# MoE experts: rows gathered one expert earlier, 16-bit splits and crossbar transfers ahead of the scatters

## The chip, the cores and the metric

The kernel runs on one core of one Trainium2 chip. The metric is the device time of the slowest core in microseconds (us); with one core that is this core's time. Times in the text are us.

## What is computed

Banded attention (4 batches, 8 heads, 768 positions, head size 64) feeds a mixture of 8 experts over the 3072 tokens that result. The attention part stands outside the change; the expert part is this, shortened:

```python
logits = x @ w_gate                       # x: (3072, 512)
expert_idx = np.argmax(logits, axis=1)    # one expert for each token
for i in range(N):                        # a list of tokens for each expert
    e = expert_idx[i]
    if counts[e] < capacity:
        disp[e, counts[e]] = x[i]
        ...
h = np.maximum(np.einsum('ecd,edf->ecf', disp, w1), 0.0)   # 512 -> 1024
y = np.einsum('ecf,efd->ecd', h, w2)                       # 1024 -> 512
out[i] = gate_w[i] * y[expert_idx[i], pos[i]]              # back to the token's row
```

## The kernel before

The attention's rows are written to memory (`xrows`), the router makes for each expert a list of the tokens that chose it, and the experts 0 to 7 then run one after the other. All float32 products are made of float32r halves: a tensor t is split into th (rounded) and tl = t - th, and a product is three matmuls (th*wh, th*wl, tl*wh).

**Rounds.** An expert is a loop over f = 0 to 7, called rounds here, each with 128 of the 1024 hidden units. TensorE does in round f first the second layer of round f - 2 (`second`, lines 739 to 741: three matmuls of 512 columns for each block of 128 tokens), then the first layer of round f (`layer1`, line 731: 12 matmuls, as wide as the expert has tokens, in steps of 32). Which width runs is decided on the chip by branches (`widths`, line 940); all engines pass these branches. Widths are 480, 416, 384, 416, 384, 416, 416 and 288 for the experts 0 to 7. Where the last block holds only 32 tokens, eight small matmuls (`beside`, line 955) do its second layer, half of them in round 5 and half at the end. What is left of an expert's second layer (`last`) runs in round 0 of the next expert: 18 matmuls of 512 columns for three whole blocks (24 for four), and the eight small ones.

**ScalarE and VectorE** work in the order written, for each round: `hidden` (hh, line 981 on ScalarE; hl, line 982 on VectorE; hr, line 984), then pieces, the splits of weights that are used two steps later (a step is two rounds; lines 141 and 142: a cast of ScalarE and a subtraction of VectorE; four in round 1, two in each of the rounds 2 to 7), then in the rounds 3 to 6 a `join` for one block of 128 token rows of the next expert: x (line 853, VectorE), xh (line 855, ScalarE), xl (line 856, VectorE). The next expert's first layer needs all four xh.

**The rows of the next expert.** `gather` makes four blocks. `fetch` issues four indirect transfers on GpSimd's queue (xg, line 345). `halves` then splits the float32 rows into 16-bit halves on GpSimd (flat, line 847, two buffers) and issues a crossbar transfer on SyncE's queue (DMA transpose, line 848) that writes them turned back into xg. There are four xg buffers. For the experts 2 to 7 all of that is written in round 1 of the expert before, with a `drain` of GpSimd (line 1032) between the four gathers and the four splits. Expert 1's rows are gathered in round 2 of expert 0, expert 0's by another way.

**Queues.** The order on all five engines is the order written (manual schedules), so GpSimd's and SyncE's queues are served in order. GpSimd's: the four scatters of the expert before (out_dram, line 871, written in round 0), the four gathers, the drain, the four splits. SyncE's: `fetch(step + 3)` at the start of each even round loads 1 MB of weights (four transfers of 256 KB, line 133: two of w1, called wr, with four buffers, and two of w2, called w2r), and the crossbar transfers stand between the loads of round 0 and those of round 2.

Of the kernel before, what the change touches and what calls it, by code (L numbers as in the profile page):

```python
# [11 lines left out]
F32R = mybir.dt.float32r  # L12
# [8 lines left out]
P = 128  # L21
# [8 lines left out]
def fused(ctx: ExitStack, tc, q, k, v, wg, w1, w2, out, shape, n_global, n_local, cap):  # L30
    nc = tc.nc
    B, H, S, D = shape
    DM, E = wg.shape
# [4 lines left out]
    KC = DM // P  # L38
    NF = FF // P
# [71 lines left out]
    T4 = FIXED * P  # L111
# [219 lines left out]
    def turn_rows(ps, rows):  # L331
        for c in range(KC):
            nc.tensor.transpose(ps[:, c, :], rows[:, c * P:(c + 1) * P], ident)
# [9 lines left out]
    def fetch_rows(pool, name, bufs, gi, n=N):  # L343
        xg = pool.tile([P, DM], F32, name=name, bufs=bufs)
        ld = nc.gpsimd.indirect_dma_start(out=xg, out_offset=None, in_=xrows[0:n],  # L345
                                          in_offset=bass.IndirectOffsetOnAxis(ap=gi.bitcast(U32), axis=0),
                                          bounds_check=n - 1, oob_is_err=False)
        return xg, ld
# [385 lines left out]
    def layer2(e, f, a, y, hh, hl):  # L734
        w = wparts[e * (NF // FP) + f // FP][1]
        w2h, w2l = w["h"], w["l"]
        t = slice(a * P, (a + 1) * P)
        fi = f % FP
        nc.tensor.matmul(y, hh[:, t], w2h[:, fi], start=f == 0, stop=False)  # L739
        nc.tensor.matmul(y, hh[:, t], w2l[:, fi], start=False, stop=False)  # L740
        nc.tensor.matmul(y, hl[:, t], w2h[:, fi], start=False, stop=f == NF - 1)  # L741
# [46 lines left out]
    gi = const.tile([P, E, FIXED], I32, name="gi")  # L788
# [5 lines left out]
    def list_rows():  # L794
        nc.vector.tensor_copy(tb.bitcast(I32)[:, :, :, 0].rearrange("p e a -> p (e a)"), held[:, 0])
        nc.vector.tensor_copy(tb[:, :, :, 1].rearrange("p e a -> p (e a)"), held[:, 1])
# [20 lines left out]
    def bankC():  # L817
        spare.append(spare.pop(0) or bank([P, DM]))
        return spare[-1]
# [3 lines left out]
    moe = mctx.enter_context(tc.tile_pool(name="moe", bufs=2))  # L823

    def gather(gi, rows=()):

        xh, xl = [moe.tile([P, KC, T4], F32R, name=n) for n in ("xh", "xl")]
        rows = list(rows)

        def fetch():  # L830
            for a in range(len(rows), FIXED):
                xg, ld = fetch_rows(moe, "xg", FIXED, gi(a))
                rows.append(xg)
            return ld

        def turn(a, ps=None):
            ps = (bankC() if ps is None else ps).rearrange("p (c t) -> p c t", c=KC)
            turn_rows(ps, rows[a])
            o = slice(a * P, (a + 1) * P)
            nc.scalar.copy(xh[:, :, o], ps)  # L840
            nc.vector.tensor_tensor(xl[:, :, o], ps, xh.bitcast(F32)[:, :, o], op=ALU.subtract)

        def halves(a):


            flat = moe.tile([P, 2 * DM], U16, name="flat")
            nc.gpsimd.tensor_copy(flat.rearrange("p (n f) -> p n f", n=2), rows[a].bitcast(U16).rearrange("p (f n) -> p n f", n=2))  # L847
            nc.sync.dma_start_transpose(out=rows[a].bitcast(U16).rearrange("p (c t) -> p c t", t=P), in_=flat)

        def join(a):  # L850
            o = slice(a * P, (a + 1) * P)
            x = moe.tile([P, KC, P], F32, name="x")
            nc.vector.tensor_copy(x.bitcast(U16).rearrange("p c (t n) -> p n c t", n=2),  # L853
                                  rows[a].bitcast(U16).rearrange("p (n c t) -> p n c t", n=2, t=P))
            nc.scalar.copy(xh[:, :, o], x)  # L855
            nc.vector.tensor_tensor(xl[:, :, o], x, xh.bitcast(F32)[:, :, o], op=ALU.subtract)
        return xh, xl, turn, fetch, halves, join

    out_scatters = []

# [72 lines left out]
    def widths(e):  # L933

        def among(lo, hi):
            if hi - lo == 1:
                yield FINE * (lo + FIRST_ARM)
                return
            mid = (lo + hi) // 2
            with tc.If(arms[e] > mid - 1) as more:  # L940
                yield from among(mid, hi)
            with more.Else():
                yield from among(lo, mid)
        yield from among(0, NV)
# [13 lines left out]
    def whole(w):  # L958

        return range(SURE, w // P + (w % P > 2 * GR))  # L960
# [7 lines left out]
    def fetch(step, after=()):  # L968
        if step < STEPS and step not in wparts:
            pieces[step] = raw_weights(step, moe, "wr", 4, after, plain)  # L970
# [18 lines left out]
    def load_arm(e):  # L989
        arms[e] = nc.values_load(arm[0:1, e:e + 1], engines=[PE], min_val=0, max_val=NV - 1)  # L990


    xs = gather(lambda a: gi[:, 0, a:a + 1], first["rows"])
    fetch(PREFETCH)
    got = xs[3]()
    first["rest"]()
    for t, n in zip(xs, ("xh", "xl")):
        nc.gpsimd.tensor_copy(t[:, :, START], first[n])
# [17 lines left out]
    for e in range(E):  # L1016
        xh, xl = xs[0:2]
        hs = hs0 if e == 0 else {}

        def second(fs, a, e=e, hs=hs):  # L1020
            for f in fs:
                layer2(e, f, a, y_ps[a], *hs[f][0:2])

        for f in range(NF):
            step = (e * NF + f) // FP
            if f % FP == 0:
                fetch(step + SPLIT + 1)
                split = pieces.pop(step + SPLIT, [])
            if f == 1 and 0 < e < E - 1:
                xs = gather(lambda a, e=e: gi[:, e + 1, a:a + 1])  # L1030
                xs[3]()
                nc.gpsimd.drain()  # L1032
                for a in range(FIXED):
                    xs[4](a)
            if f == 1 and e == E - 1:
                nc.gpsimd.drain()
                most = nc.values_load(nblk[:, E:E + 1], min_val=0, max_val=max(RB, FIXED + 1))
            if f == 2 and e == 0:
                xs = gather(lambda a, e=e: gi[:, e + 1, a:a + 1])
                xs[3]()  # L1040
                for a in range(FIXED):
                    xs[4](a)
                first["h"](first["held"])
                list_rows()
            if f == 4 and e + 1 < E:
                load_arm(e + 1)
            h = h_ps[f % 2]

            fs = (f - 2,) if f > 1 else ()
            for a in range(SURE):  # L1050
                second([i for i in fs if e > 0 or i >= EARLY], a)
            part = slice(FIRST * P if e == 0 and f < EARLY else 0, T4)
            for w in widths(e) if e > 0 or f > 1 else ():
                for a in whole(w):
                    second(fs, a)
                if f == 5:
                    beside(e, range(0, 4), w, hs)
                layer1(e, f, h, xh, xl, slice(part.start, w))
            hidden(hs, f, part)
            if f == 0 and last is not None:  # L1060
                last()
            if f == 3 and e == 0:
                to = take_beside(tb)
            if f == 5 and e == 1:
                count_blocks()
            for piece in () if f == 0 else split if f == 1 else split[2 * (f % FP):2 * (f % FP) + 2]:
                piece()

            turned = {4: (0,), 5: (1, 2), 6: (3,)} if e == 0 else {3: (0,), 4: (1,), 5: (2,), 6: (3,)}
            for a in turned.get(f, ()) if e + 1 < E else ():  # L1070
                xs[5](a)

        def last(e=e, second=second, hs=hs):
            for a in range(SURE):
                second((NF - 2,), a)
            for w in widths(e):
                beside(e, range(4, NF), w, hs)
                for a in whole(w):
                    second((NF - 2, NF - 1), a)
            rest = [finish(e, a, to[:, e, a - SURE], y_ps[a]) for a in range(SURE, FIXED)]  # L1080
            rest[0]()
            for a in range(SURE):
                second((NF - 1,), a)
                finish(e, a, first["tb"][:, a] if e == 0 and a < FIRST else tb[:, e, a], y_ps[a])()
            rest[1]()
# [127 lines left out]
```

## Time and profile before

| what | value |
|---|---|
| median of 3 runs | 528.46 us (528.44, 528.46, 533.24) |
| the profiled execution | 525.51 us, span 523.8 us |
| busy share of the span | TensorE 85%, VectorE 59%, ScalarE 55%, GpSimd 34% |
| mean granted TensorE clock | 0.957 |
| matmuls | 3943 |

The span is the time from the first to the last instruction of the profiled execution; 1.7 us of its time lie around it. Engines are named PE (TensorE), DVE (VectorE), ACT (ScalarE), POOL (GpSimd) and SP (SyncE) in the rows; a q behind a name is that engine's queue. Matmul records overlap, since matmuls are pipelined: the pace is read from start to start. A granted clock of 1.00 is 2.4 GHz, one of 0.50 is 1.2 GHz.

### The profile page before, as it was taken

The numbers are of one execution on the slowest core, as the hardware profiler recorded it, in microseconds if no ns is written. First come the engines' busy times: TensorE is split into PE (matmuls) and PEld (weight loads), VectorE is DVE, ScalarE is ACT, GpSimd is POOL, SyncE is SP. The second block draws the span as 40 slices with busy tenths as digits, with TensorE's granted clock in tenths as the row PEclk, the third lists the DMA queues.
The fourth block names the chain that finished last, engine by engine and source line by source line (L and its number), as shares of the span: only waits on it lengthen the run. The fifth ranks groups of instructions, "written<-read, shape, count | busy, mean of one in ns | idle before, by whom it ended". The sixth has DMA issues, their size and how long they took to land.

```text
span 523.8 us, 11549 instructions
## 1 busy us (share of the span) xinstructions
PE 447.7 (85%) x3943; PEld 367.3 (70%) x3943; DVE 308.1 (59%) x978; ACT 287.2 (55%) x799; POOL 178.7 (34%) x285
## 2 busy tenths in 40 slices
PE   6899999999998889959977897798579958986993
PEld 3777787877787778847865795677469746955781
DVE  6679899898764564436534551663365355516632
ACT  4989999998733345335523551562356245515642
POOL 6004456665347104410640162054106301530303
PEclk9999999999999999988996999799889979998998
DMA  9999689763349833484459338635843572376301
GB/s 253 303 339 300 201 235 310 227 202 98 103 145 288 175 109 112 122 201 167 136 83 256 109 117 145 215 132 104 217 147 125 92 253 103 128 127 217 130 6 51
DMA packets 79601, 88.79 MB, mean 170 GB/s; under 512 B 35537, under 2 KB 47825, under 8 KB 79476
## 3 DMA queue, kind: packets, MB, share of 16 engines
q1 hardware_dynamic: 73812, 72.31, 49.1%
q0 software_dynamic: 5120, 14.69, 8.8%
q8 instruction: 92, 1.51, 1.2%
q14 instruction: 33, 0.27, 0.2%
q10 hardware_dynamic: 544, 0.02, 0.1%
HBM read 67.06 MB, written 14.68 MB: 156 GB/s over the span
## 4 chain that ended last, share of the span: by engine, by line
issue 35%; PE 27%; POOL 11%; DMA 10%; DVE 7%; ACT 6%; POOLq 2%; SPq 2%; ACTq 0%; DVEq 0%
DMA xg<-flat 6%; POOL flat L847 4%; POOL xg L345 4%; PE bank L731 4%; PE bank L486 4%; PE bank L548 4%; PE bank L545 4%; DVE sc L462 3%; PE bank L524 2%; ACT sc L497 2%; DMA wr<-in_moe_w_dram 2%; POOLq L1032 2%; POOL out_dram L871 2%; PE bank L739 2%; PE bank L741 1%
## 5 line engine op out<-in xcount | busy, mean ns | idle before, releaser
L739 PE MATMUL bank<-w2h,hh 128*128 128x512 f32 x192 | 83.1, 433 | 41.1 <-ACT hh L981 37.8
L731 PE MATMUL bank<-xh,w1h 128*128 128x416 f32 (+5 forms) x272 | 92.4, 347 | 10.0 <-ACT xh L855 9.6
L731 PE MATMUL bank<-xh,w1l 128*128 128x416 f32 (+5 forms) x272 | 90.7, 341 | 0.0
L497 ACT ACTIVATE sc<-sc,mx 128x168 f32<-128x168 f32 (+1 forms) x192 | 80.1, 422 | 10.6 <-DVE mx L462 9.6
L871 POOL DMA_INDIRECT out_dram<-ysb,to x16 | 16.2, 1012 | 197.5 <-ACT ysb L863 195.1
L741 PE MATMUL bank<-w2h,hl 128*128 128x512 f32 x192 | 81.3, 423 | 1.3 <-DVE hl L982 0.5
L740 PE MATMUL bank<-w2l,hh 128*128 128x512 f32 x192 | 80.8, 421 | 0.0
L739 PEld LDWEIGHTS bank<-w2h,hh 128*128 128x128 f32 x192 | 38.5, 200 | 55.9 <-ACT hh L981 41.9
L142 DVE TENSOR_TENSOR w1l<-wr,w1h 128x512 fp32r<-128x512 f32 x58 | 38.1, 692 | 61.1 <-ACT w1h L141 58.2
L731 PEld LDWEIGHTS bank<-xh,w1h 128*128 128x128 f32 x272 | 53.6, 197 | 19.4 <-ACT xh L855 11.0
L982 DVE SCALAR_TENSOR_TENSOR hl<-bank,hh 128x512 fp32r<-128x512 f32 (+1 forms) x64 | 42.9, 670 | 28.5 <-ACT hh L981 27.5
L731 PE MATMUL bank<-xl,w1h 128*128 128x416 f32 (+5 forms) x272 | 57.3, 334 | 0.0
L981 ACT ACTIVATE hh<-bank 128x512 fp32r<-128x512 f32 (+1 forms) x64 | 37.3, 583 | 35.9 <-PE bank L731 29.5
L855 ACT CAST xh<-x 128x512 fp32r<-128x512 f32 x28 | 17.4, 620 | 70.6 <-DVE x L853 70.6
L462 DVE CUSTOM_DVE_ANT_0 sc<-bank,bias 128x168 f32<-128x168 f32 (+1 forms) x192 | 49.1, 321 | 11.5 <-PE bank L486 10.6
L731 PEld LDWEIGHTS bank<-xh,w1l 128*128 128x128 f32 x272 | 52.9, 194 | 3.0
L984 ACT ACTIVATE hr<-bank 128x256 f32<-128x256 f32 x64 | 24.6, 385 | 52.5 <-DVE hl L982 48.0
L141 ACT CAST w1h<-wr 128x512 fp32r<-128x512 f32 x58 | 33.4, 617 | 32.9 <-DMA wr<-in_moe_w_dram 32.8
L847 POOL COPY flat<-xg 128x1024 uint16<-128x1024 uint16 x28 | 35.3, 1280 | 46.8 <-DMA xg<-flat 24.1
L142 DVE TENSOR_TENSOR w2l<-w2r,w2h 128x512 fp32r<-128x512 f32 x58 | 39.1, 716 | 19.2 <-ACT w2h L141 19.2
L741 PEld LDWEIGHTS bank<-w2h,hl 128*128 128x128 f32 x192 | 38.8, 202 | 15.4 <-DVE hl L982 5.7
L731 PEld LDWEIGHTS bank<-xl,w1h 128*128 128x128 f32 x272 | 47.2, 188 | 0.6
(174 smaller groups left out, 796.5 us busy)
## 6 DMA issues: line engine op xcount, KB each, us to landing
wr<-in_moe_w_dram SPq DMA_DIRECT2D x58, 256.0 KB
w2r<-in_moe_w_dram SPq DMA_DIRECT2D x58, 256.0 KB
K<-in_k_dram SPq DMA_DIRECT2D x24, 272.0 KB
Q<-in_q_dram SPq DMA_DIRECT2D x24, 256.0 KB
v<-in_v_dram SPq DMA_DIRECT2D x24, 256.0 KB
xrows<-xr SPq DMA_DIRECT2D x23, 256.0 KB
v<-in_v_dram SPq DMA_DIRECT2D x20, 208.0 KB
wst<-in_moe_w_dram SPq DMA_DIRECT2D x12, 256.0 KB
```

The lines of the kernel that those rows point to most:

```text
L141: nc.scalar.copy(parts["h"][:, s], r)
L142: (nc.gpsimd if meanwhile else nc.vector).tensor_tensor(parts["l"][:, s], r, parts["h"].bitcast(F32)[:, s], op=ALU.subtract)
L462: nc.vector.tensor_tensor_reduce(out=un["sc"][:, a, HQ:HQ + un["w"]], in0=un["ps"][hh][:, gg, :], in1=un["bias"][:, 4 * (u % 2) + a, :], s ...
L497: un["e"] = nc.scalar.activation(sc[:, a, HQ:HQ + w], sc[:, a, HQ:HQ + w], AF.Exp, bias=un["mx"][:, a:a + 1], scale=-1.0, accum_out=sm[:, ...
L731: nc.tensor.matmul(to, ww[:, c, fs], xx[:, c, s], start=n == 0, stop=n == 3 * KC - 1)
L739: nc.tensor.matmul(y, hh[:, t], w2h[:, fi], start=f == 0, stop=False)
L740: nc.tensor.matmul(y, hh[:, t], w2l[:, fi], start=False, stop=False)
L741: nc.tensor.matmul(y, hl[:, t], w2h[:, fi], start=False, stop=f == NF - 1)
L847: nc.gpsimd.tensor_copy(flat.rearrange("p (n f) -> p n f", n=2), rows[a].bitcast(U16).rearrange("p (f n) -> p n f", n=2))
L871: w = nc.gpsimd.indirect_dma_start(out=out, out_offset=bass.IndirectOffsetOnAxis(ap=rows.bitcast(U32)[:, 0:1], axis=0), in_=ysb, in_offset ...
L981: nc.scalar.activation(hh[:, s], h[:, s], AF.Relu)
L982: nc.vector.scalar_tensor_tensor(hl[:, s], h[:, s], 0.0, hh.bitcast(F32)[:, s], op0=ALU.max, op1=ALU.subtract)
```

## The change

`gather` no longer takes the two tiles xh and xl at once; `place` does that later. In the last round of expert e the four row blocks of expert e + 2 are gathered (for e = 0 to 5). In round 0 of expert e + 1 the splits and crossbar transfers of these rows are written, ahead of that round's scatters. The drain stays in round 1; gathers and splits are now written outside that round. Expert 1's rows and the joins keep their place.

```diff
@@ -824,8 +824,13 @@
 
     def gather(gi, rows=()):
 
-        xh, xl = [moe.tile([P, KC, T4], F32R, name=n) for n in ("xh", "xl")]
+        xh = xl = None
         rows = list(rows)
+
+        def place():
+            nonlocal xh, xl
+            xh, xl = [moe.tile([P, KC, T4], F32R, name=n) for n in ("xh", "xl")]
+            return xh, xl
 
         def fetch():
             for a in range(len(rows), FIXED):
@@ -854,7 +859,7 @@
                                   rows[a].bitcast(U16).rearrange("p (n c t) -> p n c t", n=2, t=P))
             nc.scalar.copy(xh[:, :, o], x)
             nc.vector.tensor_tensor(xl[:, :, o], x, xh.bitcast(F32)[:, :, o], op=ALU.subtract)
-        return xh, xl, turn, fetch, halves, join
+        return place, None, turn, fetch, halves, join
 
     out_scatters = []
 
@@ -993,6 +998,7 @@
     xs = gather(lambda a: gi[:, 0, a:a + 1], first["rows"])
     fetch(PREFETCH)
     got = xs[3]()
+    xs = xs[0]() + xs[2:]
     first["rest"]()
     for t, n in zip(xs, ("xh", "xl")):
         nc.gpsimd.tensor_copy(t[:, :, START], first[n])
@@ -1026,18 +1032,23 @@
             if f % FP == 0:
                 fetch(step + SPLIT + 1)
                 split = pieces.pop(step + SPLIT, [])
-            if f == 1 and 0 < e < E - 1:
-                xs = gather(lambda a, e=e: gi[:, e + 1, a:a + 1])
-                xs[3]()
-                nc.gpsimd.drain()
+            if f == 0 and 0 < e < E - 1:
+                xs = on
+                xs = xs[0]() + xs[2:]
                 for a in range(FIXED):
                     xs[4](a)
+            if f == 1 and 0 < e < E - 1:
+                nc.gpsimd.drain()
+            if f == NF - 1 and e + 2 < E:
+                on = gather(lambda a, e=e: gi[:, e + 2, a:a + 1])
+                on[3]()
             if f == 1 and e == E - 1:
                 nc.gpsimd.drain()
                 most = nc.values_load(nblk[:, E:E + 1], min_val=0, max_val=max(RB, FIXED + 1))
             if f == 2 and e == 0:
                 xs = gather(lambda a, e=e: gi[:, e + 1, a:a + 1])
                 xs[3]()
+                xs = xs[0]() + xs[2:]
                 for a in range(FIXED):
                     xs[4](a)
                 first["h"](first["held"])
```

On GpSimd's queue the stretch between expert 1's and expert 2's scatters read as follows before (xg are the gathers, flat the splits, out_dram the scatters; L940 are the passed branches; what an instruction waits for stands in brackets, DMASW and DMAHW being transfers of GpSimd's and SyncE's queue):

```order
L871 DMA out_dram<-ysb,tb 3072x512 [waits DMASW2_49,Activation_49]
L940 UNCONDITIONAL_BRANCH
L871 DMA out_dram<-ysb,to 3072x512 [waits DMASW3_49,DVE_49]
L345 DMA xg<-xrows,gi 128x512 x2
L345 DMA xg<-xrows,gi 128x512 [waits DMAHW7_49,Pool_49]
L345 DMA xg<-xrows,gi 128x512 [waits DMAHW0_49,Pool_49]
L940 UNCONDITIONAL_BRANCH x2
L847 COPY flat<-xg 128x1024 [waits DMASW4_49]
L847 COPY flat<-xg 128x1024 [waits DMASW5_49]
L940 UNCONDITIONAL_BRANCH
L847 COPY flat<-xg 128x1024 [waits DMAHW1_49,DMASW6_49,Pool_49]
```

And now, from the gathers to the scatters (L945 are the branches):

```order
L345 DMA xg<-xrows,gi 128x512 [waits DVE_49] x2
L945 UNCONDITIONAL_BRANCH
L345 DMA xg<-xrows,gi 128x512 [waits DMAHW7_49,DVE_49,Pool_49]
L345 DMA xg<-xrows,gi 128x512 [waits DMAHW0_49,DVE_49,Pool_49]
L852 COPY flat<-xg 128x1024 [waits DMASW0_49]
L852 COPY flat<-xg 128x1024 [waits DMASW1_49]
L945 UNCONDITIONAL_BRANCH x3
L852 COPY flat<-xg 128x1024 [waits DMAHW1_49,DMASW2_49,Pool_49]
L945 UNCONDITIONAL_BRANCH
L852 COPY flat<-xg 128x1024 [waits DMAHW2_49,DMASW3_49,Pool_49]
L876 DMA out_dram<-ysb,to 3072x512 [waits DMASW4_49,Activation_49]
```

The gathers moved from behind the scatters to before the splits of the next expert's start, each behind a wait on VectorE (the x of the block whose xg buffer it takes), and the scatters moved behind the splits. The order does not list the drain.

SyncE's queue for the same stretch, before (wr and w2r are the loads of weights):

```order
L133 DMA w2r<-in_moe_w_dram 128x512 x2
L940 UNCONDITIONAL_BRANCH x7
L848 DMA_TRANSPOSE xg<-flat 128x8x128 x2
L940 UNCONDITIONAL_BRANCH
L848 DMA_TRANSPOSE xg<-flat 128x8x128 x2
L133 DMA wr<-in_moe_w_dram 128x512 x2
```

and now:

```order
L133 DMA w2r<-in_moe_w_dram 128x512 x2
L945 UNCONDITIONAL_BRANCH x3
L853 DMA_TRANSPOSE xg<-flat 128x8x128 x2
L945 UNCONDITIONAL_BRANCH x2
L853 DMA_TRANSPOSE xg<-flat 128x8x128 x2
L945 UNCONDITIONAL_BRANCH
L133 DMA wr<-in_moe_w_dram 128x512 x2
```

The order of the transfers is the same; the crossbar transfers stand fewer branches (rounds) after the loads of round 0. On PE, DVE and ACT the order of the instructions is unchanged.

## Rows read from the trace of the kernel before

**Rows 1.** Waits: engine, line waited for, total us, times, longest us.

```profile
PE bank L739 <- ACT hh L981: 37.8, 9, 6.0
...
PE bank L731 <- ACT xh L855: 9.6, 4, 2.9
```

**Rows 2.** Timeline of PE: first matmul of experts 1, 3, 5, 7 (start, duration).

```profile
195.12 0.46 PE L731 MATMUL bank<-xh,w1h 128*128 128x416 f32 x1 [1.67 <-ACT xh L855]
...
291.68 0.46 PE L731 MATMUL bank<-xh,w1h 128*128 128x416 f32 x1 [2.60 <-ACT xh L855]
...
387.42 0.46 PE L731 MATMUL bank<-xh,w1h 128*128 128x416 f32 x1 [2.90 <-ACT xh L855]
...
481.58 0.37 PE L731 MATMUL bank<-xh,w1h 128*128 128x288 f32 x1 [0.32 <-ACT hr L984]
```

**Rows 3.** Timeline of PE: full rounds of expert 1, then of expert 2.

```profile
207.47 0.35 PE L731 MATMUL bank<-xh,w1h 128*128 128x416 f32 x1
...
209.74 0.40 PE L739 MATMUL bank<-w2h,hh 128*128 128x512 f32 x1
...
211.85 0.35 PE L731 MATMUL bank<-xh,w1h 128*128 128x416 f32 x1
...
220.70 1.06 PE L955 MATMUL bank<-w2r,hr 128*32 128x512 f32 x8
...
253.98 0.34 PE L731 MATMUL bank<-xh,w1h 128*128 128x384 f32 x1
...
256.06 0.39 PE L739 MATMUL bank<-w2h,hh 128*128 128x512 f32 x1
```

**Rows 4.** Timeline of PE: the wait in round 7 of expert 1.

```profile
234.72 0.79 PE L739 MATMUL bank<-w2h,hh 128*128 128x512 f32 x1 [5.50 <-ACT hh L981]
```

**Rows 5.** Timelines of ACT and DVE in expert 1: the waits behind that.

```profile
222.15 0.76 DVE L853 COPY x<-xg 128x1024 uint16<-128x1024 uint16 x1 [4.20 <-DMA xg<-flat]
...
230.62 0.62 ACT L141 CAST w1h<-wr 128x512 fp32r<-128x512 f32 x1 [5.19 <-DMA wr<-in_moe_w_dram]
```

**Rows 6.** Timeline of SP's queue in expert 1.

```profile
218.87 8.25 SPq L848 DMA_TRANSPOSE xg<-flat  x4
227.22 1.71 SPq L133 DMA_DIRECT2D wr<-in_moe_w_dram  x2
```

**Rows 7.** Timeline of POOL in expert 1; then the drain's six (min/median/max ns).

```profile
208.10 1.43 POOL L345 DMA_INDIRECT xg<-xrows,gi  x1 [0.30 <-issue]
...
217.71 2.12 POOL L847 COPY flat<-xg 128x1024 uint16<-128x1024 uint16 x2 [3.81 <-issue]
...
L1032 POOLq DRAIN  x6: 9290/9714/10738, 207.8 to 447.6; - x6
```

**Rows 8.** Windows: busy us of PE, PEld, DVE, ACT, POOL; granted clock; DMA share, GB/s.

```profile
234.70:239.40 4.70, 4.68 (x11) 3.65 (x12) 3.84 (x15) 2.22 (x5) 0.00 (x0) 0.50 0.83 314
...
387.40:396.30 8.90, 8.88 (x43) 8.02 (x44) 5.31 (x8) 5.20 (x10) 2.05 (x2) 1.00 0.36 122
272.10:275.60 3.50, 3.32 (x9) 2.37 (x10) 0.86 (x2) 0.38 (x1) 1.17 (x1) 0.72 0.83 144
```

**Rows 9.** Timeline of ACT in expert 2: rounds with a join, one after the other.

```profile
286.13 0.62 ACT L855 CAST xh<-x 128x512 fp32r<-128x512 f32 x1 [1.50 <-DVE x L853]
286.65 0.59 ACT L981 ACTIVATE hh<-bank 128x512 fp32r<-128x512 f32 x1
...
291.01 0.62 ACT L855 CAST xh<-x 128x512 fp32r<-128x512 f32 x1 [1.49 <-DVE x L853]
```

**Rows 10.** Timeline of PE: another wait in expert 2.

```profile
272.13 0.51 PE L739 MATMUL bank<-w2h,hh 128*128 128x512 f32 x1 [3.34 <-ACT hh L981]
```

**Rows 11.** Timelines of DVE and POOL in expert 2: splits that met.

```profile
259.14 1.29 DVE L142 TENSOR_TENSOR w1l<-wr,w1h 128x512 fp32r<-128x512 f32 x2 [0.96 <-ACT w1h L141]
...
263.66 2.13 DVE L142 TENSOR_TENSOR w2l<-w2r,w2h 128x512 fp32r<-128x512 f32 x2 [0.96 <-ACT w2h L141]
...
263.89 2.80 POOL L847 COPY flat<-xg 128x1024 uint16<-128x1024 uint16 x2 [3.19 <-issue]
```

## The prediction

> **What bounds the kernel now.** I read the waits of PE first, because PE is the busiest engine: it waited 37.8 us for hh and 9.6 us for xh [rows 1]. Then PE's timeline from the first matmul of expert 1 to that of expert 7, which is 481.58 - 195.12 = 286.46 us for six experts, 47.7 each [rows 2]. Against that stands what PE needs when nothing holds it. A round with 416 tokens takes 211.85 - 207.47 = 4.38 us, 2.27 of it first layer (207.47 to 209.74) and 2.11 nine matmuls of the second. With 384 tokens the first layer takes 2.08 (253.98 to 256.06), a round 4.19. The eight small matmuls take about 1.0 [rows 3]. An expert is two first layers without a second layer (rounds 0 and 1), six full rounds, and the 18 matmuls left over (4.22). So 416 tokens need 2 x 2.27 + 4.22 + 6 x 4.38 = 35.0, and 384 need 2 x 2.08 + 4.22 + 6 x 4.19 = 33.5; each expert of 416 adds 1.0 in its own round 5 and 1.0 in the expert that follows; expert 1 carries 1.4 more, as expert 0 leaves 24 matmuls. Experts 1, 3, 5, 6 (416) and 2, 4 (384), with three of the small groups at the ends of 1, 3 and 5 in the next expert, sum to 4 x 36.0 + 2 x 33.5 + 3 x 1.0 + 1.4 = 215.4 us. **About 71 us of the six experts are lost.**
>
> Where: in expert 1 PE stands 5.50 us for hh before round 7's second layer [rows 4] and then runs at a granted clock of 0.50, which is 1.2 GHz, for 4.7 us [rows 8], which costs another 2.35. Behind it two engines wait in the order written [rows 5]: VectorE 4.20 us for the crossbar transfer of the first block (round 3), then ScalarE 5.19 us for wr, the weights to be split in round 4. SP's queue says why they are late: the load of wr is issued at 227.22, directly behind four crossbar transfers that held the queue from 218.87 [rows 6]. These wait for the splits, which begin at 217.71, and those stand behind the gathers, issued from 208.10 on, and the drain, which lasts some 9.7 us six times [rows 7]. The gathers in turn stood behind the scatters. So the chain is scatters, gathers, drain, splits, crossbar, weights, hh, and it runs into the next expert's xh (waits of 2.60 and 2.90 us at the starts of experts 3 and 5) [rows 2].
>
> **The change, part by part.** Call T the end of round 7's first layer.
>
> *Gathers in round 7.* Their GpSimd time is the same, 1.0 to 1.46 each. New is a wait on VectorE: a block's gather needs the x of the block that held its xg buffer. The joins stand in rounds 3 to 6, so three gathers go out before round 7 and the last about 0.7 us after T. Queued behind that wait are only other gathers and the next splits; no one waits for those yet. Cost on the path: nothing.
>
> *Splits and crossbar before the scatters.* The first split now begins at about T + 2; from first split to free SP queue took 227.22 - 217.71 = 9.5 us [rows 6, 7], so the weights of round 2 can be issued at T + 11.5. T to the end of round 1's first layer is about 11, so the queue is free when round 2 starts, and round 4, which splits these weights, is 8.8 us further. Before, the same point came 8.7 us behind round 3's first layer (211.85 + 4.38 + 2.27 = 218.5) [rows 3]. The crossbar transfers are all issued at T + 11.5, while round 3's join begins at about T + 23. Both waits of [rows 5] go: the 4.20 and the 5.19, and with them the 5.50 of PE and the slow clock. *Scatters* wait now for the fourth split, to about T + 10, some us later than before; they free ysb for the next expert's end, 25 us on: nothing. *The drain* comes behind the scatters with nothing urgent behind it until the gathers in round 4: nothing.
>
> *What is late next.* The join itself. In expert 2, with all data there, ScalarE and VectorE go through a round with a join in 291.01 - 286.13 = 4.88 us [rows 9], longer than PE's 4.38 or 4.19. Rounds 3 to 6 have joins. With 416 tokens the lag is 0.5 at round 4, is eaten by the small matmuls of round 5, and is 0.5 again at round 6; with 384 it grows to 3 x 0.69 = 2.1. From the start of hh to that of xh are 291.01 - 286.65 = 4.36, xh takes 0.62, and hh starts 0.1 after its first layer. So the last xh is there 0.1 + 0.5 + 4.36 + 0.7 = 5.7 us after round 6's first layer ends (384: 7.3), while PE wants it after 4.2 (384: 4.05). The start of the next expert waits 1.5 us behind each expert of 416 and 3.2 behind one of 384: 4 x 1.5 + 2 x 3.2 = 12.4 us that the change leaves.
>
> **The sum.** The six experts take 215.4 + 12.4 = 227.8 instead of 286.5: 58.7 less. Expert 0 and expert 7 keep their times. The profiled execution, 525.5 us, would become 466.8; the runs' median lies 3.0 above it, so 528.46 - 58.7 = 469.8. I take **470**.
>
> **Unknown costs.** First, the clock. A wait of 2.90 was followed by a stretch at 1.00 [rows 2, 8], one of 3.34 by one at 0.72 [rows 8, 10]. The 3.2 us behind experts 2 and 4 lie between; the rows count a wait from the modelled end of a matmul, which overlaps the next by some 0.1 to 0.2 us, so they would show 3.0 to 3.1, a little nearer to 2.90: I take 0 for the forecast and keep two slow stretches of 2.35, 4.7 us, for the range. Second, splits that meet: a pair of VectorE's took 2.13 instead of 1.29 where GpSimd split rows, and GpSimd's pair 2.80 instead of 2.12 [rows 7, 11]. The splits now stand in rounds 7 to 1. At most two such pairs an expert, 1.7 us, 10 in all if it were on the path; VectorE has no join there, so I take 0. Third, all 12.4 us might be hidden after all: 457, the floor.
>
> The Trainium skill, "SBUF — State Buffer", section "Who interferes with whom", has a rule that speaks against the second point: a VectorE instruction with two SBUF inputs and a GpSimd instruction that reads SBUF lock each other out for a whole instruction. This trace agrees in kind: 0.84 us more for two [rows 11]. By that rule four whole splits of about 1.05 could block VectorE in each expert, 25 us in all on the path, and the time would be 495.
>
> **The rivals.**
> 1. *Meetings and clock.* The splits hold up VectorE in round 7 so that the last xl, hl and the four splits of round 1 come late, and the longer starts drop the clock. For it: [rows 11]. Against it: the first split follows a gather that itself waits for the last x, so the last xl (0.7 us) is nearly through. Price 4.7 + 10: 484.
> 2. *Half the gain.* Weights stay late for another reason: gathers now run beside the weight loads of rounds 4 and 6, and the crossbar transfers beside that of round 0. For it: DMA engines were 0.83 busy in the burst after the wait [rows 8]. Against it: that burst exists because the queue was held, and the loads now spread. If a third to a half of the 7.85 us of PE stays per expert plus some start waits, about 25 us come back: 495.
> 3. *Slower: a closed ring.* The last gather waits for the last x, the splits and crossbar for that gather, the weights for the crossbar, the joins for the weights' splits, and the last x stands behind those. The ring from x to x: gather 1.4, splits and crossbar 9.5, load 3.4 (227.22 to 230.62) [rows 5, 6], the rounds 4 to 6 at 4.88 each 14.6: 29 us. It sets the pace only above the 38 us of an expert, and makes the kernel slower only above 47.7, when crossbar and loads take 19 us more, for instance because gathers and weights fill the DMA engines. At 50 us for six experts: 528.5 + 6 x 2.3 = 542. Nothing in the rows comes near.
> 4. *It doesn't do it.* The order shows the gathers ahead of the splits and the scatters behind; but if the drain came to stand between gathers and splits, 9.7 us more would pass. Even then SP is free at T + 21, about 1 us past round 3's first layer, against 8.7 before. No change would need waits of [rows 5] that have another cause than the queue: 528.
>
> **How the numbers follow.** Forecast 0.68, own range 460 to 480; rival 1 0.15; rival 2 0.10; rival 3 0.03; rival 4 0.04. The range 459 to 488 holds the forecast and rival 1, and leaves out rivals 2 to 4, 0.17. A change of 1% (5 us) is about what a measurement of this kernel can tell from none. Faster by over 1%: 0.68 + 0.15 + 0.10 = 0.93; the same 0.04; slower 0.03.
>
> **What the new profile would show.** Right: the six waits of PE for hh gone, the waits of the first layer for xh at the starts of experts 2 to 7 as its only large ones, 1.5 and 3.2 us in turn; six experts in 225 to 235 us; the granted clock near 1.00 from 195 us on; no wait of ScalarE for wr and of VectorE for the crossbar. Wrong: if wr is still waited for in round 4, the queue was not the cause; if the starts wait over 3.3 us and the clock halves behind them, rival 1; if the last gather's wait on VectorE shows up in SP's queue past round 2, rival 3.

## The result and the profile after

| | before | after |
|---|---|---|
| median (range), 4 runs each | 529.47 us (528.44 to 533.24) | 469.24 us (466.78 to 472.68) |
| profiled execution, span | 525.51, 523.8 | 468.36, 466.6 |
| six experts (first matmul of expert 1 to that of 7) | 286.46 | 228.49 |
| mean granted TensorE clock | 0.957 | 0.981 |

The ratio is 0.886, 95% interval 0.878 to 0.893. The forecast was 470, with 227.8 for the six experts.

Windows of the six experts, before and then after (columns as in [rows 8]). Of the 58.0 us, 40.4 are idle time of PE (47.2 before, 6.8 after); the other 17.6 are PE's busy time, which fell from 239.22 to 221.65 for the same matmuls, at a mean granted clock of 0.93 before and 0.98 after.

```profile
195.12:481.58 286.46, 239.22 (x1070) 198.03 (x1071) 139.93 (x216) 122.71 (x238) 84.99 (x72) 0.93 0.56 152
```

```profile
196.07:424.56 228.49, 221.65 (x1070) 191.59 (x1071) 145.74 (x219) 122.65 (x239) 78.63 (x69) 0.98 0.70 187
```

The waits of PE after (columns as in [rows 1]): those for hh are gone from the view, and what is left at this place is xh. No wait of ScalarE for wr and none of VectorE for the crossbar is in the list ([rows 5] showed one of each; before they came to 32.8 and 26.9 us).

```profile
PE bank L731 <- ACT xh L860: 8.4, 4, 3.0
```

PE's timeline after, with the first matmul of each of the experts 1 to 7 (start, duration, then in brackets the idle time ahead). Against [rows 2] only three of the starts behind expert 1 have a wait, those of the experts 3, 5 and 6.

```profile
196.07 0.46 PE L731 MATMUL bank<-xh,w1h 128*128 128x416 f32 x1 [1.60 <-ACT xh L860]
...
233.67 0.34 PE L731 MATMUL bank<-xh,w1h 128*128 128x384 f32 x1
...
271.49 0.72 PE L731 MATMUL bank<-xh,w1h 128*128 128x416 f32 x1 [2.64 <-ACT xh L860]
...
309.11 0.33 PE L731 MATMUL bank<-xh,w1h 128*128 128x384 f32 x1
...
346.93 0.71 PE L731 MATMUL bank<-xh,w1h 128*128 128x416 f32 x1 [2.98 <-ACT xh L860]
...
387.19 0.46 PE L731 MATMUL bank<-xh,w1h 128*128 128x416 f32 x1 [1.21 <-ACT xh L860]
...
424.56 0.29 PE L731 MATMUL bank<-xh,w1h 128*128 128x288 f32 x1
```

SP's queue after, at the starts of the experts 1 and 2. In [rows 6] the crossbar transfers came 23.75 us behind the first matmul of expert 1 (218.87 - 195.12) and the weights for round 4 at 32.1; now they come at 2.6 and 13.5.

```profile
198.69 9.74 SPq L853 DMA_TRANSPOSE xg<-flat  x4
209.58 0.93 SPq L133 DMA_DIRECT2D wr<-in_moe_w_dram  x2
...
237.83 9.55 SPq L853 DMA_TRANSPOSE xg<-flat  x4
247.47 1.14 SPq L133 DMA_DIRECT2D wr<-in_moe_w_dram  x2
```

POOL's timeline after, from the last gather of expert 1 on: the splits stand directly behind it and ahead of the scatters, where [rows 7] had the drain between.

```profile
235.24 1.51 POOL L345 DMA_INDIRECT xg<-xrows,gi  x1 [3.39 <-issue]
236.75 2.02 POOL L852 COPY flat<-xg 128x1024 uint16<-128x1024 uint16 x2
242.95 2.02 POOL L852 COPY flat<-xg 128x1024 uint16<-128x1024 uint16 x2 [4.17 <-DMA xg<-flat]
245.13 1.04 POOL L876 DMA_INDIRECT out_dram<-ysb,to  x1 [0.15 <-issue]
```

Windows of the span after (columns as in [rows 8]): the clock is full from the start of expert 1 to that of expert 3, and falls behind the two long starts.

```profile
196.00:271.40 75.40, 72.78 (x358) 62.83 (x358) 49.27 (x79) 40.95 (x82) 27.55 (x24) 1.00 0.75 195
271.50:275.00 3.50, 3.50 (x12) 3.40 (x13) 2.54 (x3) 1.84 (x4) 3.48 (x3) 0.59 0.81 286
347.00:351.30 4.30, 4.30 (x13) 4.10 (x14) 3.35 (x4) 1.78 (x4) 3.50 (x3) 0.50 0.90 272
351.30:356.00 4.70, 4.70 (x19) 3.75 (x18) 1.05 (x2) 1.99 (x4) 1.04 (x1) 0.83 0.70 123
```

### The profile page after: what moved, and what is told of

It reads as the page before. It is cut to its first block, busy times and chain, and to the rows that moved or that the text cites. A ratio compares the mean times of both kernels' runs of the same rounds, so it can differ in the third digit from the quotient of the medians.

```text
span 466.6 us, 11549 instructions
## 1 busy us (share of the span) xinstructions
PE 431.5 (92%) x3943; PEld 361.8 (78%) x3943; DVE 312.6 (67%) x978; ACT 286.7 (61%) x799; POOL 175.4 (38%) x285
## 4 chain that ended last, share of the span: by engine, by line
PE 60%; DVE 12%; issue 8%; DMA 8%; ACT 8%; SPq 2%; POOL 1%; POOLq 0%; DVEq 0%; ACTq 0%
PE bank L731 21%; PE bank L739 7%; PE bank L740 6%; PE bank L741 6%; PE bank L486 4%; PE bank L548 4%; PE bank L545 4%; PE bank L524 3%; DMA w2r<-in_moe_w_dram 3%; DVE sc L462 2%; DMA K<-in_k_dram 2%; DVE x L858 2%; ACT xh L860 2%; DVE hl L987 2%; PE bank L960 2%
## 5 line engine op out<-in xcount | busy, mean ns | idle before, releaser
L345 POOL DMA_INDIRECT xg<-xrows,gi x30 | 36.6, 1221 | 119.1 <-DVE x L858 76.3
L739 PE MATMUL bank<-w2h,hh 128*128 128x512 f32 x192 | 77.6, 404 | 3.4 <-ACT hr L989 3.2
L741 PE MATMUL bank<-w2h,hl 128*128 128x512 f32 x192 | 76.1, 396 | 0.3 <-DVE hl L756 0.3
L740 PE MATMUL bank<-w2l,hh 128*128 128x512 f32 x192 | 76.3, 398 | 0.0
L731 PEld LDWEIGHTS bank<-xh,w1h 128*128 128x128 f32 x272 | 52.3, 192 | 18.5 <-ACT xh L860 9.8
L987 DVE SCALAR_TENSOR_TENSOR hl<-bank,hh 128x512 fp32r<-128x512 f32 (+1 forms) x64 | 42.9, 670 | 27.4 <-ACT hh L986 25.7
L142 DVE TENSOR_TENSOR w2l<-w2r,w2h 128x512 fp32r<-128x512 f32 x58 | 44.7, 811 | 19.2 <-ACT w2h L141 17.2
L739 PEld LDWEIGHTS bank<-w2h,hh 128*128 128x128 f32 x192 | 36.4, 189 | 14.9 <-issue 5.5
L741 PEld LDWEIGHTS bank<-w2h,hl 128*128 128x128 f32 x192 | 36.2, 189 | 9.4 <-DVE hl L756 0.7
L740 PEld LDWEIGHTS bank<-w2l,hh 128*128 128x128 f32 x192 | 36.4, 190 | 5.9
L852 POOL COPY flat<-xg 128x1024 uint16<-128x1024 uint16 x28 | 28.6, 1041 | 32.8 <-DMA xg<-flat 32.8
```

Source lines behind the costliest of these rows:

```text
L142: (nc.gpsimd if meanwhile else nc.vector).tensor_tensor(parts["l"][:, s], r, parts["h"].bitcast(F32)[:, s], op=ALU.subtract)
L731: nc.tensor.matmul(to, ww[:, c, fs], xx[:, c, s], start=n == 0, stop=n == 3 * KC - 1)
L987: nc.vector.scalar_tensor_tensor(hl[:, s], h[:, s], 0.0, hh.bitcast(F32)[:, s], op0=ALU.max, op1=ALU.subtract)
```

## The experiments

Four theories stand in the expectations. **A**: the loss hangs on when the crossbar transfers are done in SyncE's queue and let the weights for round 4 through. **B**: the early gather is the gain. **C**: the drain ahead of the splits is what cost. **D**, later: waits of PE behind branches take the place of waits for xh.

The table sums up ten runs' profiles beside before and after. Crossbar and weights are the times at which SP's queue begins the first and the issue for round 4, counted from expert 1's first matmul; the next column is the six experts; the last two are the summed waits of VectorE for the crossbar and of ScalarE for wr. Each ratio is against the kernel before as measured beside that run (medians of 530.4 to 532.4 us beside e1 to e10), so a difference of 2 or 3 us between the medians of different rows can't be told from none.

| run | median us | ratio (95%) | crossbar | weights | six experts | VectorE | ScalarE |
|---|---|---|---|---|---|---|---|
| before | 529.47 | 1 | 23.8 | 32.1 | 286.5 | 26.9 | 32.8 |
| e2 drain behind splits | 515.11 | 0.971 (0.964 to 0.978) | 19.9 | 29.5 | 274.1 | 14.1 | 32.9 |
| e3 loads first | 509.57 | 0.962 (0.955 to 0.969) | 25.7 | 13.5 | 266.2 | 36.4 | 0 |
| e10 loads first, drain behind | 487.00 | 0.914 (0.908 to 0.920) | 19.9 | 13.5 | 244.0 | 12.7 | 0 |
| e1 gather early only | 495.33 | 0.936 (0.929 to 0.944) | 16.2 | 25.3 | 251.6 | 0 | 15.2 |
| e9 weights late only | 494.87 | 0.927 (0.920 to 0.935) | 2.6 | 26.0 | 252.9 | 0 | 24.2 |
| e6 early gather, drain behind | 481.68 | 0.903 (0.897 to 0.909) | 15.3 | 23.6 | 237.1 | 0 | 0 |
| e5 drain between | 469.48 | 0.881 (0.877 to 0.885) | 7.0 | 15.2 | 229.8 | 0 | 0 |
| after | 469.24 | 0.886 (0.878 to 0.893) | 2.6 | 13.5 | 228.5 | 0 | 0 |
| e4 joins in rounds 2 to 5 | 468.38 | 0.883 (0.876 to 0.889) | 2.6 | 13.5 | 229.1 | 0 | 0 |
| e8 no branches | 463.85 | 0.873 (0.868 to 0.878) | 2.6 | 15.1 | 228.8 | 0 | 0 |
| e7 joins early, no branches | 457.74 | 0.860 (0.856 to 0.864) | 2.6 | 15.1 | 220.1 | 0 | 0 |

**e1: the early gather alone.** The changed kernel, with splits and drain back in round 1, behind the scatters.

```diff
-            if f == 0 and 0 < e < E - 1:
+            if f == 1 and 0 < e < E - 1:
                 xs = on
                 xs = xs[0]() + xs[2:]
+                nc.gpsimd.drain()
                 for a in range(FIXED):
                     xs[4](a)
-            if f == 1 and 0 < e < E - 1:
-                nc.gpsimd.drain()
```

> The changed kernel with the splits and crossbar transfers put back into round 1, behind the scatters and the drain; only the gathers are early. Theory A (the loss is set by when the crossbar transfers leave SyncE's queue and let the weights of round 4 through): without the gathers in between, the drain should end about 6 us sooner than before, so the weights of round 4 are issued about 6 us sooner, ScalarE still waits some 3 us for them, TensorE little in round 7 and about 3 us more at the starts of experts 3, 5 and 6: 480 to 490. Theory B (the early gather itself is the gain, its place ahead of the scatters is not): 469, as the changed kernel. Theory C (the drain ahead of the splits is the loss): 520 or more, since the drain stays ahead of the splits.

495.33 us: 34 of the 60 us. B falls, since the early gather alone leaves 26 us on the table. So does C as the whole cause (it asked for 520 or more), since the drain stands ahead of the splits and more than half of the gain is there. A's number is missed by 5 us. The wait that is left is the one for wr, in the waits of ACT:

```profile
ACT w1h L141 <- DMA wr<-in_moe_w_dram: 15.2, 10, 2.7
```

**e2: the drain alone.** The kernel before, drain behind the splits.

```diff
                 xs[3]()
-                nc.gpsimd.drain()
                 for a in range(FIXED):
                     xs[4](a)
+                nc.gpsimd.drain()
```

> The kernel before with the drain of round 1 moved behind the four splits; gathers stay in round 1. Theory A: the first split starts some 3 to 4 us sooner (when its gather has landed, not when the drain is over), the weights of round 4 come as much sooner, and TensorE's wait in round 7 falls from 5.5 to 1 or 2 us: 495 to 505. Theory B (early gather is the gain): 525 to 530. Theory C (the drain is the loss): close to the changed kernel, 470 to 480.

515.11 us, between A and B and far from C's 470 to 480. The drain of 9.7 us [rows 7] moved the crossbar by only 3.9 (23.75 to 19.85) and the weights by 2.6. The drain's record begins at 207.8, ahead of the gathers, so most of it passes while GpSimd issues these; only the 3.81 us ahead of the first split in [rows 7] are its own. In e2 the split follows the last gather without a gap (POOL's timeline):

```profile
214.00 1.00 POOL L345 DMA_INDIRECT xg<-xrows,gi  x1 [0.30 <-issue]
215.01 2.02 POOL L847 COPY flat<-xg 128x1024 uint16<-128x1024 uint16 x2
```

**e3: weights ahead of the crossbar.** The kernel before, gather and splits one round later, so that the weights for round 4 stand ahead in SP's queue.

```diff
-            if f == 1 and 0 < e < E - 1:
+            if f == 2 and 0 < e < E - 1:
```

> The kernel before with gathers, drain, splits and crossbar transfers written in round 2 instead of 1, so that on SyncE's queue the weights of round 4 are issued ahead of the crossbar transfers; GpSimd's order is unchanged. Theory A: ScalarE's wait for wr in round 4 goes; VectorE's wait of about 4 us for the first crossbar transfer in round 3 stays, and with it a lag that reaches TensorE's round 7 by 1 to 2 us and the next expert's start by some 4 us more: 490 to 500. Theory B (only late rows count, the weights' wait is a follower): 515 to 528.

509.57 us, between A and B. ScalarE's wait for wr is gone, but VectorE's for the crossbar grew from 26.9 to 36.4; its timeline in expert 1 (against 4.20 in [rows 5]):

```profile
225.35 0.74 DVE L853 COPY x<-xg 128x1024 uint16<-128x1024 uint16 x1 [7.53 <-DMA xg<-flat]
```

So the queue's lateness costs twice: by the weights behind the crossbar and by the crossbar itself. A's forecast kept the crossbar's wait at some 4 us an expert, as before; it grew to 6.1 on average (36.4 in six), and the forecast missed by 10 us.

**e10: the same, with the crossbar sooner.** As e3, with the drain behind the splits too (both diffs above).

> The kernel before, with the gather and the splits one round later (so that the weights of round 4 are issued ahead of the crossbar transfers, as in e3) and with the drain behind the splits, so that these end some 3.7 us sooner; the gather isn't early. Theory A: VectorE's wait for the crossbar falls from some 6 us to about 2 us an expert, and the median is 480 to 495 us. If the drain is irrelevant here: 505 to 510 us, as e3.

487.00 us, within A's range and well off e3: crossbar 5.9 us sooner, 22.2 us less in the six experts, with gathers as late as before. The waits of VectorE:

```profile
DVE x L853 <- DMA xg<-flat: 12.7, 6, 2.7
```

**e9: weights late only.** The changed kernel; the loads that stand in round 4's split are held until that round's hr is done.

```diff
-            nc.scalar.activation(hr, h[:, SURE * P:], AF.Relu)
+            return nc.scalar.activation(hr, h[:, SURE * P:], AF.Relu)
...
-            if f % FP == 0:
+            inner = 0 < e < E - 1
+            if f % FP == 0 and not (inner and f in (2, 4)):
                 fetch(step + SPLIT + 1)
+            if f % FP == 0 and not (inner and f == 4):
                 split = pieces.pop(step + SPLIT, [])
...
-            hidden(hs, f, part)
+            held_by = hidden(hs, f, part)
+            if f == 4 and inner:
+                fetch(step + SPLIT, (held_by,))
+                split = pieces.pop(step + SPLIT, [])
+                fetch(step + SPLIT + 1)
```

> The changed kernel, in which only the loads of the next expert's weights that stand in round 4 are held until round 4's activation of hr is done, so that they leave SyncE's queue about where they left it before, or later; the gather, the splits and the crossbar transfers stay early. Theory A (the loss is set by when the weights come free of the queue): ScalarE's wait for wr comes back, some 3.4 us in each of six experts, and the median is 485 to 495 us. If the weights did not matter, and the crossbar transfers alone did: 469 to 472 us.

494.87 us. The wait for wr is back, at 3.5 us on average, and the time follows. Lines of the waits, then ACT's timeline in expert 1:

```profile
ACT w1h L141 <- DMA wr<-in_moe_w_dram: 24.2, 7, 5.1
...
PE bank L739 <- ACT hh L986: 8.0, 5, 3.1
...
225.71 1.27 ACT L141 CAST w1h<-wr 128x512 fp32r<-128x512 f32 x2 [4.09 <-DMA wr<-in_moe_w_dram]
```

With everything else early, late weights alone cost 24.4 us in the six experts (252.9 against 228.5). The loads that follow in SP's queue are held too, so this is the whole queue from that point. e1, with the weights as late, lands within 2 us of it (251.6).

**e6: early gather, drain behind.** As e1, with the drain behind the splits.

```diff
-                nc.gpsimd.drain()
                 for a in range(FIXED):
                     xs[4](a)
+                nc.gpsimd.drain()
```

> As the first experiment (gathers early, splits in round 1 behind the scatters), but the drain behind the splits. The first split then waits only for the four scatters, at about 8 to 13 us into the next expert; SyncE's queue is free of crossbar transfers about the end of round 2's first layer. Theory A: ScalarE waits for wr hardly (under 1 us an expert), 470 to 478; what the first experiment lost against the changed kernel (26 us) is then nearly all the drain's. If the scatters are what counts: 485 to 495, as the first experiment.

481.68 us; 3.7 us above A's range. Weights only 1.7 us sooner than in e1 are just in time: no wait for wr is left. The drain's part is 14 of the 26 us that e1 had lost, not nearly all. 8.6 us more than after remain in the six experts: PE's waits there sum to 13.5 us (9.3 of it for xh) where after had 6.8, all for xh; the other 2 aren't traced. Another 3.5 us lie ahead of expert 1 (it starts at 199.57, not 196.07).

**e5: the drain between, early splits.** The changed kernel, drain in round 0 ahead of the splits.

```diff
                 xs = xs[0]() + xs[2:]
+                nc.gpsimd.drain()
                 for a in range(FIXED):
                     xs[4](a)
-            if f == 1 and 0 < e < E - 1:
-                nc.gpsimd.drain()
```

> The changed kernel with the drain moved from round 1 to between the early gathers and the splits. The last gather ends about 1.5 us ahead of the first split, so the drain can only hold the splits some 4 us. Theory A (there are some 10 us between the end of the crossbar transfers on SyncE's queue and the need for the weights of round 4): the same within 1%, 466 to 473. Theory C (a drain ahead of the splits is what costs): 485 or more.

469.48 us: no difference from after (the intervals overlap). The weights come at 15.2, 1.7 us later; nothing waits for them. The drain costs nothing by itself, so C is out as a cause of its own. Where the splits are late, the drain's place does count, by what it delays the queue: some 14 to 23 us (e1 against e6, before against e2, e3 against e10).

**e4: joins one round earlier.** The changed kernel with

```diff
-            turned = {4: (0,), 5: (1, 2), 6: (3,)} if e == 0 else {3: (0,), 4: (1,), 5: (2,), 6: (3,)}
+            turned = {4: (0,), 5: (1, 2), 6: (3,)} if e == 0 else {2: (0,), 3: (1,), 4: (2,), 5: (3,)}
```

> The changed kernel with the joins of the experts 1 to 6 in rounds 2 to 5 instead of 3 to 6. If the waits for xh at the starts of experts 3, 5 and 6 (2.64, 2.98, 1.21 us) come from the last join standing in round 6, they go, and with them the half clock behind two of them (1.4 and 2.8 us): about 11 us less, 456 to 460. If the joined rows are then not there in time (crossbar transfers end too late for round 2), VectorE waits in round 2 and little is gained: 466 to 472.

468.38 us, no difference that can be measured. That lies in the range for rows that come too late, but VectorE has no wait for the crossbar; the reason is another. PE's waits for xh shrink to 1.3 us, and waits that nothing in the profile releases ("issue") appear, at the first matmul of the third block of the second layer, which is the first one behind the branch on the width: 6.3 us in eight waits of PE, where after has none at this line. First the weight loads of line 739 in after, then in e4 (busy, mean ns, idle before with its causes), then PE's waits in e4 and one of them in its timeline:

```profile
L739 PEld LDWEIGHTS bank<-w2h,hh 128*128 128x128 f32 x192 | 36.4, 189 | 14.9 <-issue 5.5 <-ACT hr L989 3.6
```

```profile
L739 PEld LDWEIGHTS bank<-w2h,hh 128*128 128x128 f32 x192 | 36.1, 188 | 24.9 <-issue 14.9 <-ACT w2h L141 2.5 <-ACT hr L989 1.8
...
PE bank L739 <- issue: 6.3, 8, 1.5
...
282.03 0.51 PE L739 MATMUL bank<-w2h,hh 128*128 128x512 f32 x1 [1.33 <-issue]
```

**e7 and e8: without branches.** e7 is e4 and e8 is the changed kernel, each with the widths written into the program; they serve these inputs only, and the matmuls that run are the same.

```diff
-        yield from among(0, NV)
+        yield (480, 416, 384, 416, 384, 416, 416, 288)[e]
```

> The changed kernel with joins in rounds 2 to 5, and with the branches on an expert's width replaced by the widths that these inputs lead to (480, 416, 384, 416, 384, 416, 416, 288), so that nothing branches within the experts 0 to 7; the matmuls that run are the same. Theory D (the waits of TensorE behind branches, put down to issue, are instructions that come late and took the place of the waits for xh in the fourth experiment): they go, 454 to 460. Rival (those waits have another cause, a queue or a semaphore that the profile does not show): 465 to 470.

> The changed kernel (joins in rounds 3 to 6) with the same widths written in, without branches. Theory D: the waits for xh at the starts of experts 3, 5 and 6 and the half clock behind them stay, only some 3 us of waits behind branches go: 463 to 469, that is 7 to 11 us above the kernel with early joins and no branches. Rival: no difference between the two, both 465 to 470.

e8 463.85, e7 457.74: both within D's ranges. Early joins are worth 6.1 us without branches (D had 7 to 11) and 0.9, which is no measurable difference, with them. PE has no wait for "issue" at line 739 in either. The weight loads of line 739 in e7:

```profile
L739 PEld LDWEIGHTS bank<-w2h,hh 128*128 128x128 f32 x192 | 36.2, 189 | 10.1 <-issue 4.2
```

So the waits go with the branches. That they are late instructions is argued from this, not shown. Of the two DMA queues that carry instructions, one moves more with branches (packets, MB, share; e4, then e7). But no packet of either moves within e4's three longest waits, those that end at 282.03, 331.50 and 411.97:

```profile
q8 instruction: 92, 1.51, 1.3%
```

```profile
q8 instruction: 33, 0.54, 0.5%
```

e8's own 5.4 us against after lie in expert 0 (expert 1 starts at 192.28, not 196.07) and behind expert 7's start (40.5 against 42.0 us to the end), not in the six.

**What follows.** Loads and crossbar roughly add up: weights late alone +24.4 (e9, at 26.0), crossbar late alone +15.4 to +37.7 (e10 and e3, at 19.9 and 25.7), both late +58.0 (before, at 32.1 and 23.8). The lateness differs between these runs, so the sum is rough. A held, in a wider form than first stated: two consumers wait on one queue. For kernels that stay general, none of the variants beats the change; e7 beats both kernels at the price of fixed widths.

## Why the prediction was right, step by step

**The chain** (scatters, gathers, drain, splits, crossbar, weights, hh) held: each link that was put back alone returned part of the loss, by the wait that was named for it (e1, e9: wr; e3, e10: crossbar). One link was overrated: the drain, taken at 9.7 us, mostly passes while the gathers are issued; e2 shows 3.9 us in its place.

**Times on the queue.** The boundary T of experts 1 and 2 is 233.67. The last gather went out at T + 1.6 (0.7 was predicted), the first split at T + 3.1 (2), the weights at T + 13.8 (11.5). This 2.3 us cost nothing, as round 4's split begins without a wait at 258.40, 24.7 behind T:

```profile
258.40 1.13 ACT L141 CAST w1h<-wr 128x512 fp32r<-128x512 f32 x2
```

**The starts** were mis-sized: 12.4 us predicted, 6.8 measured (2.64 + 2.98 + 1.21). Where a wait came it fitted: 2.64 and 2.98 for 3.2 behind experts of 384, 1.21 for 1.5 behind one of 416. The step that failed is "4 x 1.5": the experts 2, 4 and 7 (384, 384 and 288 tokens) read only three blocks of 128 rows, so the last join, the fourth block's, is not needed for their first layer. The prediction took the statement that a first layer needs all four xh for every width. ACT's timeline after shows it: the last xh for expert 2 begins 0.86 us behind that expert's first matmul (233.67).

```profile
234.53 0.62 ACT L860 CAST xh<-x 128x512 fp32r<-128x512 f32 x1 [1.51 <-DVE x L858]
```

**The clock** was taken at 0 and 4.7 kept for the range. It cost some 4.2: the first layer from 271.49 to 275.16 took 3.67 us instead of the 2.27 of [rows 3], 1.4 more, and the stretch from 346.93 on some 2.8 more. So the two errors nearly cancel: 215.4 + 6.8 + 4.2 is 226.4, and 2.1 us in small pieces up to 228.5 aren't traced. The right total owes something to that.

**Splits that meet** were there as feared, but off PE's path. VectorE's timeline in round 7 of expert 1, against 1.29 for a pair in [rows 11]:

```profile
237.44 2.50 DVE L142 TENSOR_TENSOR w2l<-w2r,w2h 128x512 fp32r<-128x512 f32 x2 [0.96 <-ACT w2h L141]
```

The pair takes 1.2 us more while GpSimd splits rows (236.75 to 238.77), and no wait of PE follows at 233 to 240. The Trainium skill, "SBUF — State Buffer", section "Who interferes with whom", has the two engines locking each other out in such a case; the trace agrees in kind. The 25 us that the rule would have cost on the path didn't come.

**The rivals.** Half the gain: the extra load on the DMA engines (0.75 busy from 196 to 271) kept nothing late. The closed ring: no wait for wr or the crossbar is left, so it isn't the pace. Of rival 1 the slower clock came, behind waits under its 3.3 us, and at 4.2 us in all. The drain point of rival 4 is confirmed by e5: between gathers and splits it cost nothing that can be measured, and moved the weights by 1.7 us, not 9.7.

## What to carry to other kernels

In a queue that is served in order, ask of each slow entry who is queued behind it, and of each of them when its data are wanted: here crossbar transfers issued 21 us later delayed two consumers on two engines, and either one alone kept a quarter to two thirds of the loss. Being early gains nothing more once the data come before they are wanted (weights at 13.5 or 15.2 us give the same time, at 23.6 no wait for them is left, at 26 they cost 24 us). When a wait at a boundary is estimated, check for each case of a variable size whether the consumer really reads the last piece.

## What was not expected of the hardware

**The same wait may or may not slow TensorE.** Behind waits of 2.60 and 2.90 us before [rows 2] the clock stayed at 1.00 (below, and [rows 8]), behind 2.64 and 2.98 after it fell to 0.59 and 0.50.

```profile
291.70:300.00 8.30, 8.30 (x40) 7.44 (x41) 4.71 (x8) 5.15 (x10) 1.67 (x2) 1.00 0.37 121
```

The length doesn't decide: in e8 two waits of 2.98 at the same place of two experts went either way. PE's timeline and the windows behind, in e8:

```profile
269.36 0.45 PE L731 MATMUL bank<-xh,w1h 128*128 128x416 f32 x1 [2.98 <-ACT xh L860]
...
343.39 0.71 PE L731 MATMUL bank<-xh,w1h 128*128 128x416 f32 x1 [2.98 <-ACT xh L860]
...
269.40:278.00 8.60, 8.60 (x41) 7.75 (x42) 5.96 (x8) 5.03 (x10) 4.11 (x4) 1.00 0.95 194
343.40:347.70 4.30, 4.30 (x12) 4.12 (x13) 3.34 (x4) 1.84 (x4) 3.53 (x3) 0.50 0.89 275
```

In e9 even 2.02 us was followed by 0.54, in e1 3.01 us by 1.00:

```profile
364.20 0.47 PE L731 MATMUL bank<-xh,w1h 128*128 128x416 f32 x1 [2.02 <-ACT xh L860]
...
364.30:368.00 3.70, 3.70 (x12) 3.53 (x13) 2.74 (x3) 1.75 (x4) 3.46 (x3) 0.54 0.86 287
```

```profile
365.04 0.45 PE L731 MATMUL bank<-xh,w1h 128*128 128x416 f32 x1 [3.01 <-ACT xh L860]
...
365.10:367.40 2.30, 2.30 (x12) 2.29 (x13) 1.34 (x3) 1.44 (x4) 1.49 (x1) 1.00 0.83 285
```

What decides stays open here. For an estimate it means that a wait of 2 to 3 us on TensorE carries a chance of 1.4 to 2.8 us more behind it, as the two in after show.

**Branches can hold TensorE.** Where the data are early enough, the first matmul behind a branch waits up to 1.5 us for nothing that the profile shows (e4: eight waits of PE at line 739, 6.3 us in all; none in after, and none without branches in e7 and e8). What is waited for stays open. In after the waits for xh may hide this: in e4 nearly all of these are gone, and the time is the same.
